# A causal convolution and a spectral mix: seven weight groups ahead, tail channels of two batches on two row tiles, T copies on two engines, one store per row block of four batches

## The chip, the cores and the metric

The kernel runs on one core of a Trainium2 chip. The metric is the device time of one launch in microseconds. Before, it was 216.48 us in the median of three runs, from 214.84 to 218.25. The profiled execution took 218.14 us as a run and spans 216.4 us from its first to its last instruction.

## The reference

```python
# x: (8, 3264, 192) f32; weight: (8, 7); moe_w_r, moe_w_i: (64, 192, 192); moe_w_ch: (192, 192)
w = softmax(weight, axis=-1)
x_unf = zero_pad_front(x, 6)[:, idx, :].reshape(B, S, 7, 8, 24)
x = einsum('hk,bskhg->bshg', w, x_unf).reshape(B, S, D)       # causal convolution over seven rows
X = rfft(x, axis=1)[:, :64]
Y = X @ (w_r + 1j * w_i)                                      # one 192 x 192 matrix for each of 64 modes
u = x + irfft(Y, n=S, axis=1)
out = u + maximum(u @ w_ch, 0)
```

Both Fourier transforms are done as matmuls with matrices of sines and cosines, since only 64 modes are kept.

## The kernel before

The sequence of 3264 rows is cut into 27 windows of 122 rows; a tile has 128 partitions, of which 122 are a window's own rows. `x_all` holds all eight batches and all windows in bf16. The program is written out in the order in which each engine shall work; no scheduler moves it.

**First stage, to about 75 us.** POOL's queue loads x, 24 loads (L63), casting to bf16, and behind them `w_ch` and the first weight groups. For each batch and each third of its windows `conv_unit` convolves with a banded matrix on PE (L237) and copies back into `x_all` on ACT (L244) or DVE (L246). `dft_unit` (L296) sums the 64 modes over the windows, and `xtrans` (L308, two column tiles of 64) turns the result for the mixing, into `xt`.

**Second stage, to about 121 us.** The 64 modes are mixed in 16 groups of four (loop at L367). A group's weights `wt`, real and imaginary, are two loads of 288 KB (L221) from POOL into a pool of three buffers. For each g, twelve matmuls on four column tiles (L373) give `yp`, ACT copies it to `ymix` (L379), POOL is told to load group g+3 into the buffer that has come free, then `t_next` puts one or two T units on PE and DVE, and the two transposes `et` (L387) and DVE's copy (L388) write `yeT`.

A T unit turns a third of a batch's `x_all` so that channels lie on partitions, as the last stage needs it, into `cT`. The 192 channels don't fit 128 partitions: slots alternate between channels 0 to 127 of one window, of the next, and a slot with the 64 tail channels of both, which `make_tail` (L253 to L256, DVE) has copied side by side. Up to eight transposes (L283) fill a PSUM tile, and DVE copies it out (L285), twice per unit. 24 units are spread by `2 - g % 2` over the groups, and what is left is done after g = 14 (L390), ahead of the last mix. `g_part` (L348, ACT L349) does the same for the inverse transform's matrix `gst`.

**Last stage.** For each pair of batches `zwi_pair` multiplies `yeT` by `win0` and `win1`, whose first 192 columns are `w_ch` and whose last 192 are the identity. `group_z` forms u @ w_ch for two windows and two batches in a PSUM tile of two banks (`zp`): two matmuls of 384 columns from `gst` (L422), four of 192 columns from the main channels (L427), four from the tail channels (L429). The tail matmul contracts over all 128 rows, half of which meet the zeros in `wB0` or `win1`. ACT applies the relu in place (L432). Two groups later `group_y` adds y = irfft(Y) by two more matmuls (L437) and DVE adds x (L441) into `t`, from a pool of four. A `t` has four windows of two batches, so two groups, and SP stores it, one store for each batch (L456). Windows overlap by six rows of which a later store brings the right values, so the last round's rows are cut exactly, into two pieces each. There are 80 stores; SP waits for the eighth before to land.

Of the kernel before, what the change touches and what calls it, by code (L numbers as in the profile page):

```python
# [18 lines left out]
def kernel(  # L19
# [9 lines left out]
    nc = tc.nc  # L29
# [11 lines left out]
    PAIRS = NWIN // 2  # L41
    NSLOT = 3 * PAIRS + 2
# [7 lines left out]
    USLOTS = ((0, 15), (15, 12), (27, 14))  # L50
# [35 lines left out]
    cband = ep.tile([P, H, P], BF16, tag="cband")  # L86
    fst = ep.tile([P, NWIN, 2 * MODES], BF16, tag="fst")
    xt = ep.tile([P, 4, 2 * B, MODES], BF16, tag="xt")
    sel = ep.tile([P, 2, P], BF16, tag="sel")
# [125 lines left out]
    wp = early_stack.enter_context(tc.tile_pool(name="wts", bufs=3, side="right"))  # L215
    wtiles = {}

    def load_weights(g):
        wt = wp.tile([P, MG, 3, D], BF16, tag="wt", name="wt")
        for half, src in ((0, moe_w_r), (1, moe_w_i)):  # L220
            nc.gpsimd.dma_start(out=wt[64 * half:64 * half + 64, :, :, :],  # L221
                                in_=src[MG * g:MG * g + MG, :, :].rearrange("m (p j) e -> p m j e", j=3))
        wtiles[g] = wt

    for g in range(3):
        load_weights(g)
    workp = early_stack.enter_context(tc.tile_pool(name="work", bufs=2, side="right"))
# [20 lines left out]

    def make_tail(b, u):
        w0, n = UNITS[u]  # L250
        tl = workp.tile([P, 10, D - P], BF16, tag="tail")
        if u < 2:
            nc.vector.tensor_copy(out=tl[0:WIN, 0:n, :], in_=x_all[0:WIN, b, w0:w0 + n, P:D])  # L253
        else:
            nc.vector.tensor_copy(out=tl[0:WIN, 0:n - 1, :], in_=x_all[0:WIN, b, w0:w0 + n - 1, P:D])
            nc.vector.tensor_copy(out=tl[0:WIN, n - 1:n + 1, :], in_=x_all[0:WIN, b, w0 + n - 2:w0 + n, P:D])  # L256
        return tl

    def slot_lhsT(b, u, tl, slot):
        i, r = divmod(slot, 3)  # L260
        w0 = UNITS[u][0]
        if i == PAIRS:
            if r == 0:
                return x_all[0:WIN, b, NWIN - 1, 0:P]
            j = NWIN - 1 - w0
        elif r < 2:
            return x_all[0:WIN, b, 2 * i + r, 0:P]
        else:
            j = 2 * i - w0
        return tl[0:WIN, j:j + 2, :].rearrange("p w e -> p (w e)")  # L270

    def slot_of(w):
        if w == NWIN - 1:
            return NSLOT - 2, NSLOT - 1, 1
        return 3 * (w // 2) + w % 2, 3 * (w // 2) + 2, w % 2

    def t_unit(b, u, tl):
        s0, n = USLOTS[u]
        h1 = (n + 1) // 2
        for a, cnt in ((s0, h1), (s0 + h1, n - h1)):  # L280
            tp = ptr.tile([P, 8 * WIN], BF16, tag="tp")
            for k in range(cnt):
                nc.tensor.transpose(tp[:, WIN * k:WIN * k + WIN], slot_lhsT(b, u, tl, a + k),  # L283
                                    ident[0:WIN, 0:WIN])
            nc.vector.tensor_copy(out=cT[:, b, WIN * a:WIN * (a + cnt)], in_=tp[:, 0:WIN * cnt])  # L285

    xps = {}

    def dft_unit(b, u):
# [8 lines left out]
        if u == 2:  # L298
            xs = workp.tile([P, D], BF16, tag="xs")
            nc.vector.tensor_copy(out=xs[:], in_=xp[:, 0:D])  # L300
            xps[b] = xs
# [15 lines left out]
    for i, (b, u) in enumerate(units):  # L317
        conv_unit(i, b, u)
        if i == 2:
            make_f()  # L320
            setup_stack.close()
        if xq:
            xtrans(xq.pop(0))
        dq.append((b, u))
        lag = max(1, 5 - i // 4)
        while len(dq) > lag:
            db, du = dq.pop(0)
            dft_unit(db, du)
            if du == 2:
                xq.append(db)  # L330
# [7 lines left out]
    stashp = ctx.enter_context(tc.tile_pool(name="stash", bufs=1))  # L338
    cT = stashp.tile([P, B, CTW], BF16, tag="cT")
    nc.vector.memset(cT[:, :, NSLOT * WIN:CTW], 0.0)  # L340


    def g_part(g):
        tp = ptr.tile([P, 8 * WIN], BF16, tag="tp")
        c0 = 8 * g
        n = min(8, NWIN - c0)
        for k in range(n):
            nc.tensor.transpose(tp[:, WIN * k:WIN * k + WIN], fst[0:WIN, c0 + k, :], ident[0:WIN, 0:WIN])  # L348
        nc.scalar.copy(out=gst[:, WIN * c0:WIN * (c0 + n)], in_=tp[:, 0:WIN * n])  # L349


    NG4 = MODES // 4
    tunits = [(b, u) for b in range(B) for u in range(3)]
    tails = [make_tail(*tunits[0])]
    tpos = [0]

    def t_next():
        i = tpos[0]
        if i == len(tunits):
            return  # L360
        tpos[0] += 1
        if i + 1 < len(tunits):
            tails.append(make_tail(*tunits[i + 1]))
        t_unit(*tunits[i], tails[i])

    gq = list(range((NWIN + 7) // 8))
    for g in range(NG4):  # L367
        yp = pconv.tile([P, 512], F32, tag="cv", name="yp")
        for j in range(3):
            for pos in range(4):  # L370
                m = 4 * g + pos
                wt = wtiles[m // MG]
                nc.tensor.matmul(yp[32 * pos:32 * pos + 32, 0:D],  # L373
                                 xt[:, j:j + 2, :, m].rearrange("p j k -> p (j k)"), wt[:, m % MG, j, :],
                                 start=(j == 0), stop=(j == 2), tile_position=(0, 32 * pos))
        if g + 3 < NGRP:
            load_weights(g + 3)
        ymix = workp.tile([P, D], BF16, tag="ymix")
        nc.scalar.copy(out=ymix[:], in_=yp[:, 0:D])  # L379
        for _ in range(2 - g % 2):  # L380
            if g < NG4 - 1:
                t_next()
        if gq and g % 2 == 1:
            g_part(gq.pop(0))
        et = pxx.tile([P, 2, P], BF16, tag="xt", name="et")
        for t in range(2):
            nc.tensor.transpose(et[:, t, :], ymix[:, 64 * t:64 * t + P], ident[:])  # L387
        nc.vector.tensor_copy(out=yeT[:, :, 4 * g:4 * g + 4, :],  # L388
                              in_=et[:, :, :].rearrange("p t (q k) -> p t q k", q=4)[:, :, :, 0:16])
        if g == NG4 - 2:  # L390
            while tpos[0] < len(tunits):
                t_next()
    early_stack.close()
    ps1.close()


    p3 = ctx.enter_context(tc.tile_pool(name="p3", bufs=4, side="right"))
    zwip = ctx.enter_context(tc.tile_pool(name="zwip", bufs=1, side="right"))
    zwi = zwip.tile([P, B, 2, D], BF16, tag="zwi")
    pz = ctx.enter_context(tc.tile_pool(name="pz", bufs=4, space=PSUM))  # L400

    def zwi_pair(q):
        zp = pz.tile([P, 2, 512], F32, tag="z", name="zwps")
        for i in range(2):
            b = 2 * q + i
            nc.tensor.matmul(zp[:, i, 0:2 * D], yeT[:, 0, :, :].rearrange("p m (c b) -> p (m c) b", c=2)[:, :, b], win0[:], start=True, stop=False)
            nc.tensor.matmul(zp[:, i, 0:2 * D], yeT[:, 1, :, :].rearrange("p m (c b) -> p (m c) b", c=2)[:, :, b], win1[:], start=False, stop=True)
        for i in range(2):
            dst = zwi[:, 2 * q + i, :, :]
            srcv = zp[:, i, 0:2 * D].rearrange("p (t d) -> p t d", t=2)  # L410
            if i == 0:
                nc.vector.tensor_scalar(out=dst, in0=srcv, scalar1=ascale[:, 0:1], scalar2=None, op0=ALU.mult)
            else:
                nc.scalar.activation(out=dst, in_=srcv, func=ACT.Copy, scale=ascale[:, 0:1])  # L414

    wBs = (wB0[:, :], win1[:, 0:D])

    def group_z(q, ws):
        zp = pz.tile([P, 2, 512], F32, tag="z")
        for k, w in enumerate(ws):  # L420
            sa, sb, par = slot_of(w)
            nc.tensor.matmul(zp[:, k, 0:2 * D], gst[:, WIN * w:WIN * w + P], zwi[:, 2 * q:2 * q + 2, 0, :],  # L422
                             start=True, stop=False, skip_group_check=True)
            for i in range(2):
                b = 2 * q + i
                o = zp[:, k, D * i:D * i + D]
                nc.tensor.matmul(o, cT[:, b, WIN * sa:WIN * sa + P], win0[:, 0:D], start=False, stop=False,  # L427
                                 skip_group_check=True)
                nc.tensor.matmul(o, cT[:, b, WIN * sb:WIN * sb + P], wBs[par], start=False, stop=(i == 1),  # L429
                                 skip_group_check=True)  # L430
        n = len(ws)
        nc.scalar.activation(out=zp[:, 0:n, 0:2 * D], in_=zp[:, 0:n, 0:2 * D], func=ACT.Relu)  # L432
        return zp

    def group_y(q, ws, zp, t, k0):
        for k, w in enumerate(ws):
            nc.tensor.matmul(zp[:, k, 0:2 * D], gst[:, WIN * w:WIN * w + P], zwi[:, 2 * q:2 * q + 2, 1, :],  # L437
                             start=False, stop=True, skip_group_check=True)
        n = len(ws)
        step = ws[1] - ws[0] if n > 1 else 1  # L440
        nc.vector.tensor_tensor(  # L441
# [79 lines left out]
```

## Time and profile before

| stage | us | what is busy |
|---|---|---|
| convolution, DFT | 0 to 75 | transfers, 192 GB/s to 70 us |
| mixing, T transposes | 75 to 121 | transfers, 200 GB/s to 117 us |
| start of the last stage | 121 to 140 | PE 13.3 of 20 us |
| steady last stage | 140 to 190 | PE without a gap, 300 GB/s |
| last stores | 190 to 216.4 | 223 to 254 GB/s |

| group of instructions | count | mean ns |
|---|---|---|
| L427, L429 matmul, 192 columns | 432 | 249 |
| L422, L437 matmul, 384 columns | 216 | 331, 326 |
| L283 transpose | 328 | 223 |
| L285 DVE copy of T, both of a unit's halves counted | 48 | 588 |
| L349 ACT copy of gst, 976 columns | 3 | 972 |
| L432 ACT relu of a group | 52 | 795 |
| L441 DVE add of a group | 52 | 958 |
| L456 store | 80 | 432 on SP (median) |

Matmuls are pipelined: a matmul's time is its whole way through the array, and the next one starts after its columns have streamed, every 0.082 us for 192 columns. In the granted clock a 1.00 is full speed.

### The profile page before, as it was taken

The numbers are of one execution on the slowest core, as the hardware profiler recorded it, in microseconds if no ns is written. First come the engines' busy times: TensorE is split into PE (matmuls) and PEld (weight loads), VectorE is DVE, ScalarE is ACT, GpSimd is POOL, SyncE is SP. The second block draws the span as 40 slices with busy tenths as digits, with TensorE's granted clock in tenths as the row PEclk, the third lists the DMA queues.
The fourth block names the chain that finished last, engine by engine and source line by source line (L and its number), as shares of the span: only waits on it lengthen the run. The fifth ranks groups of instructions, "written<-read, shape, count | busy, mean of one in ns | idle before, by whom it ended". The sixth has DMA issues, their size and how long they took to land.

```text
span 216.4 us, 4281 instructions
## 1 busy us (share of the span) xinstructions
PE 164.1 (76%) x1706; PEld 129.4 (60%) x1706; DVE 127.2 (59%) x224; ACT 95.9 (44%) x145; POOL 53.7 (25%) x89
## 2 busy tenths in 40 slices
PE   0248489889889798786666577799999999998700
PEld 0005267869768577665555455578878877786500
DVE  7876416433344478775767414477777777777520
ACT  2693954466547213311001144466665556665400
POOL 8998533434232044442440000000000000000000
PEclk9999999999999979999999879999999999999975
DMA  2999999999999389999998002559999999986795
GB/s 22 151 174 192 192 191 194 190 193 193 193 195 177 66 113 175 192 201 206 208 199 140 0 0 65 175 168 299 301 303 292 303 303 299 304 261 203 208 256 143
DMA packets 65669, 41.35 MB, mean 191 GB/s; under 512 B 30241, under 2 KB 65649, under 8 KB 65649
## 3 DMA queue, kind: packets, MB, share of 16 engines
q0 software_dynamic: 37088, 20.14, 68.8%
q1 hardware_dynamic: 28560, 20.94, 32.2%
q8 instruction: 13, 0.21, 0.4%
q14 instruction: 8, 0.06, 0.1%
HBM read 40.31 MB, written 20.90 MB: 283 GB/s over the span
## 4 chain that ended last, share of the span: by engine, by line
PE 50%; DMA 13%; DVE 13%; ACT 10%; SPq 6%; issue 3%; POOL 1%; DVEq 0%; ACTq 0%
DMA wt<-in_moe_w_i_dram 13%; PE cp L237 8%; PE zp L422 7%; PE zp L427 7%; PE zp L429 7%; PE xp L296 6%; PE zp L437 6%; SPq L456 6%; DVE x_all L246 4%; ACT scaled L175 4%; PE tp L283 3%; ACT x_all L244 3%; PE yp L373 2%; DVE t L441 2%; DVE cT L285 2%
## 5 line engine op out<-in xcount | busy, mean ns | idle before, releaser
L441 DVE TENSOR_TENSOR t<-zp,x_all 128x768 f32<-128x768 f32 (+1 forms) x56 | 51.6, 928 | 25.7 <-PE zp L437 23.0
L432 ACT ACTIVATE zp<-zp 128x768 f32<-128x768 f32 (+1 forms) x56 | 43.2, 772 | 33.2 <-PE zp L429 33.1
L427 PE MATMUL zp<-win,cT 128*128 128x192 bf16 x216 | 45.2, 249 | 0.0
L422 PE MATMUL zp<-zwi,gst 128*128 128x384 bf16 x108 | 35.7, 331 | 7.1 <-ACT zwi L414 5.9
L244 ACT CAST x_all<-cp 122x768 bf16<-122x768 f32 (+2 forms) x32 | 26.9, 878 | 23.6 <-PE cp L237 22.9
L237 PE MATMUL cp<-x_all,cband 128*128 128x240 bf16 (+2 forms) x192 | 27.8, 288 | 7.9 <-DVE x_all L232 3.2
L285 DVE COPY cT<-tp 128x854 bf16<-128x854 bf16 (+2 forms) x48 | 26.3, 588 | 11.2 <-PE tp L283 10.6
L246 DVE CAST x_all<-cp 122x960 bf16<-122x960 f32 (+2 forms) x16 | 17.0, 1064 | 22.7 <-PE cp L237 22.7
L237 PEld LDWEIGHTS <-cband 128*128 128x128 bf16 x192 | 19.5, 109 | 15.0 <-issue 7.0
L427 PEld LDWEIGHTS <-cT 128*128 128x128 bf16 x216 | 21.4, 99 | 11.9 <-issue 8.7
L63 POOL DMA_DIRECT2D x_all<-in_x_dram x24 | 23.9, 1005 | 15.5 <-DMA x_all<-in_x_dram 15.5
L437 PE MATMUL zp<-zwi,gst 128*128 128x384 bf16 x108 | 26.6, 326 | 0.0
L429 PEld LDWEIGHTS <-cT 128*128 128x128 bf16 x216 | 21.4, 99 | 7.3 <-issue 0.5
L283 PE MATMUL tp<-ident,x_all 122*128 122x122 bf16 x216 | 22.4, 223 | 2.9 <-DVE cT L285 2.6
L296 PE MATMUL xp<-x_all,fst 122*128 122x192 bf16 (+1 forms) x216 | 23.0, 256 | 0.9 <-DVE x_all L246 0.5
L429 PE MATMUL zp<-win,cT 128*128 128x192 bf16 x112 | 23.3, 248 | 0.0
L429 PE MATMUL zp<-wB,cT 128*128 128x192 bf16 x104 | 21.9, 250 | 0.0
L283 PEld LDWEIGHTS <-x_all 122*128 122x128 bf16 x216 | 17.3, 100 | 6.5 <-issue 4.0
L379 ACT CAST ymix<-yp 128x192 bf16<-128x192 f32 x16 | 5.1, 320 | 35.5 <-PE yp L373 35.5
L283 PE MATMUL tp<-ident,tl 122*128 122x122 bf16 x112 | 20.5, 223 | 0.0
L296 PEld LDWEIGHTS <-fst 122*128 122x128 bf16 (+1 forms) x216 | 18.9, 102 | 2.2 <-DVE x_all L246 0.7
L221 POOL DMA_DIRECT2D wt<-in_moe_w_r_dram x16 | 9.8, 616 | 33.9 <-PE yp L373 27.8
(81 smaller groups left out, 154.8 us busy)
## 6 DMA issues: line engine op xcount, KB each, us to landing
out_dram<-t SPq DMA_DIRECT2D x40, 384.0 KB, 2.7
wt<-in_moe_w_r_dram POOLq DMA_DIRECT2D x16, 288.0 KB, 6.3
wt<-in_moe_w_i_dram POOLq DMA_DIRECT2D x16, 288.0 KB, 7.1
x_all<-in_x_dram POOLq DMA_DIRECT2D x8, 432.0 KB, 14.6
x_all<-in_x_dram POOLq DMA_DIRECT2D x9, 384.0 KB, 18.1
x_all<-in_x_dram POOLq DMA_DIRECT2D x7, 480.0 KB, 17.8
out_dram<-t SPq DMA_DIRECT2D x8, 288.0 KB, 2.4
out_dram<-t SPq DMA_DIRECT2D x8, 252.0 KB, 3.1
```

What stands on the lines that cost most here:

```text
L237: nc.tensor.matmul(cp[:, j, 0:GRP * n].rearrange("p (w e) -> p w e", w=n), cband[:, h, :], x_all[:, b, w0:w0 + n, GRP * h:GRP * h + GRP], ...
L244: nc.scalar.copy(out=dst, in_=srcv)
L246: nc.vector.tensor_copy(out=dst, in_=srcv)
L283: nc.tensor.transpose(tp[:, WIN * k:WIN * k + WIN], slot_lhsT(b, u, tl, a + k), ident[0:WIN, 0:WIN])
L285: nc.vector.tensor_copy(out=cT[:, b, WIN * a:WIN * (a + cnt)], in_=tp[:, 0:WIN * cnt])
L296: nc.tensor.matmul(xp[:, 0:D], fst[0:k, c, :], x_all[0:k, b, c, :], start=(c == 0), stop=(c == NWIN - 1))
L422: nc.tensor.matmul(zp[:, k, 0:2 * D], gst[:, WIN * w:WIN * w + P], zwi[:, 2 * q:2 * q + 2, 0, :], start=True, stop=False, skip_group_check ...
L427: nc.tensor.matmul(o, cT[:, b, WIN * sa:WIN * sa + P], win0[:, 0:D], start=False, stop=False, skip_group_check=True)
L429: nc.tensor.matmul(o, cT[:, b, WIN * sb:WIN * sb + P], wBs[par], start=False, stop=(i == 1), skip_group_check=True)
L432: nc.scalar.activation(out=zp[:, 0:n, 0:2 * D], in_=zp[:, 0:n, 0:2 * D], func=ACT.Relu)
L437: nc.tensor.matmul(zp[:, k, 0:2 * D], gst[:, WIN * w:WIN * w + P], zwi[:, 2 * q:2 * q + 2, 1, :], start=False, stop=True, skip_group_check ...
L441: nc.vector.tensor_tensor(out=t[:, k0:k0 + n, :].rearrange("p k (b e) -> p k b e", b=2), in0=zp[:, 0:n, 0:2 * D].rearrange("p k (b e) -> p ...
```

## The change

**Weights.** The convolution's constants get a pool of their own on the right side, freed after the first stage. The room of the setup's tiles, free after the third convolution unit, takes the T matrix of three pairs of batches (`cTa`) and a pool for four weight groups (`wts0`); with the three rotating buffers seven groups are asked for behind x. After g = 3 the four are freed for the fourth pair's matrix (`cTb`); from g = 4 on, group g+3 is loaded when mix(g) has read its buffer.

**Tail channels.** A T matrix now belongs to a pair of batches, b and b+2. It has 27 slots with the main channels of b, 27 of b+2, and 27 in which partitions 0 to 63 hold b's tail channels and 64 to 127 those of b+2. In the last stage the two are contracted as two tiles of 64 rows, each writing its own PSUM bank. The matmuls against zeros are gone.

**T copies.** A call of `t_next` does two chunks of seven or eight transposes; DVE copies the first out, ACT the second; the same for `gst`. Both, and the mixing's tiles, use one pool of four PSUM buffers. 22 calls fill g = 0 to 14.

**Last stage.** A group is one window and four batches, so that a finished `t` is one store. There are eight `t` buffers, each half as big. 54 groups, 60 stores. The first two groups' products that don't need the mixing are put ahead of its last transposes; the y and w_ch parts of the mix are made one by one, ahead of and between the first groups.

The core of the diff:

```diff
+            for g in range(4):
+                load_weights(g, wp0)
+            for g in range(4, 7):
+                load_weights(g, wp)
...
+    def t_next(avail):
...
+        for h in range(2):
+            p, k0, n = chunks[i + h]
+            tp = pt.tile([P, 1024], BF16, tag="p", name="tp")
+            for k in range(n):
+                nc.tensor.transpose(tp[:, WIN * k:WIN * k + WIN], slot_lhsT(p, k0 + k),
+                                    ident[0:WIN, 0:WIN])
+            dst = cTs[p][:, WIN * k0:WIN * (k0 + n)]
+            if h == 0:
+                nc.vector.tensor_copy(out=dst, in_=tp[:, 0:WIN * n])
+            else:
+                nc.scalar.copy(out=dst, in_=tp[:, 0:WIN * n])
...
-        if g + 3 < NGRP:
-            load_weights(g + 3)
...
+        for i in range(2):
+            for k in range(2):
+                p = 2 * h + i
+                c0 = WIN * (2 * NWIN + w)
+                nc.tensor.matmul(zp[:, k, D * i:D * i + D], cTs[p][64 * k:64 * k + 64, c0:c0 + P], wBs[k],
+                                 start=False, stop=(i == 1 and not first), skip_group_check=True,
+                                 tile_position=(64 * k, 0))
...
+        for r0, r1 in rows:
+            dst = bass.AP(tensor=out.tensor, offset=out.offset + (4 * h * S + WIN * w + r0) * D,
+                          ap=[[D, r1 - r0], [S * D, B // 2], [1, D]])
+            nc.sync.dma_start(out=dst, in_=t[r0:r1, :, :])
...
+        if g == 3:
+            wts0_stack.close()
+            cTb = ctx.enter_context(tc.tile_pool(name="stashb", bufs=1)).tile([P, CTW], BF16, tag="cTb")
+            nc.vector.memset(cTb[:, NSLOT * WIN:CTW], 0.0)
+            cTs[3] = cTb[:, :]
+        if 4 <= g and g + 3 < NGRP:
+            load_weights(g + 3, wp)
+        if not last:
+            for _ in range(1 + g % 2):
+                t_next(2 if g < 3 else 3)
+            if gq and g % 2 == 0:
+                g_part(gq.pop(0))
+        else:
+            zps = [pza.tile([P, 2, 512], F32, tag="z", name="z") for _ in range(2)]
+            for n in range(2):
+                group_ab(*seq[n], zps[n], True)
+        mix_t(g, *m)
...
+    zw_part(0, 0)
+    zw_part(0, 1)
+    for n in range(2):
+        group_g(*seq[n], zps[n], 0, False, False)
+        relu(zps[n])
+    for n in range(2):
+        zw_part(1, n)
+        finish_group(*seq[n], zps[n])
```

## The prediction, made before the changed kernel was run

> **What bounds the kernel now.** I read the slices of the page first, then the waits, the queue that issues the weights, the windows, and last the PE timeline where a tiling mode changes.
>
> ```profile
> GB/s 22 151 174 192 192 191 194 190 193 193 193 195 177 66 113 175 192 201 206 208 199 140 0 0 65 175 168 299 301 303 292 303 303 299 304 261 203 208 256 143
> ...
> q0 software_dynamic: 37088, 20.14, 68.8%
> q1 hardware_dynamic: 28560, 20.94, 32.2%
> ```
>
> A slice is 5.41 us. The row shows three stages. Up to 72 us transfers run near 192 GB/s (x, then three weight groups) while PE convolves. From 75 to 118 us thirteen more weight groups stream at about 200 GB/s, beside the T transposes. From 133 us only stores run, at about 302 GB/s. Between them lie two holes: 70 to 78 us, and 117 to 133 us, in which nothing moves at all.
>
> ```profile
> POOL wt L221 <- PE yp L373: 27.8, 12, 9.3
> ...
> PE yp L373 <- DMA wt<-in_moe_w_i_dram: 6.3, 6, 1.4
> ```
>
> ```profile
> 65.75 0.64 POOL L221 DMA_DIRECT2D wt<-in_moe_w_i_dram  x1
> 75.66 0.61 POOL L221 DMA_DIRECT2D wt<-in_moe_w_r_dram  x1 [9.26 <-PE yp L373]
> ```
>
> The first hole is the longest wait of that list: the fourth group is issued 9.26 us after the third, because its buffer is the first group's, which mixing reads at 74.8 us. From then on PE waits for weights, and POOL for PE to free a buffer.
>
> ```profile
> 72.00:74.00 2.00, 1.14 (x15) 0.91 (x15) 0.71 (x2) 0.00 (x0) 0.00 (x0) 1.00 0.13 21
> 74.00:76.00 2.00, 1.34 (x27) 1.10 (x22) 1.01 (x4) 0.32 (x1) 0.34 (x1) 0.86 0.04 8
> 76.00:78.00 2.00, 1.96 (x21) 1.76 (x18) 1.78 (x5) 0.00 (x0) 0.88 (x2) 0.50 0.44 15
> ...
> 150.00:160.00 10.00, 10.00 (x95) 8.12 (x94) 7.44 (x8) 6.07 (x8) 0.00 (x0) 1.00 0.99 301
> 160.00:170.00 10.00, 10.00 (x94) 8.00 (x93) 7.18 (x9) 6.20 (x8) 0.00 (x0) 1.00 0.99 305
> ...
> 190.00:205.00 15.00, 13.75 (x118) 10.06 (x115) 10.20 (x13) 8.26 (x12) 0.00 (x0) 1.00 0.76 223
> ```
>
> In these windows (PE, PEld, DVE, ACT, POOL busy, clock, DMA share, GB/s) the last stage is bound twice: PE is busy 10.00 of 10 us and the DMA engines 0.99 of it. From 190 us neither is full any more (0.76, 223 GB/s): the chain of waits there consists of SPq L456, the issue of 40 small stores at some 0.5 us each. PE's last matmul ends at 204.95 us, the span at 216.4, so 11.4 us of stores hang over.
>
> ```profile
> 176.20 0.16 PE zp L422
> ...
> 177.19 0.33 PE zp L437 x2
> ...
> 178.50 0.33 PE zp L437 x2
> ```
>
> The chain of waits gives the pace: L437 comes back every 1.31 us. Of this, 0.33 are the two of L437, 0.33 the two of L422, and eight matmuls of 192 columns take 0.082 each, 0.66.
>
> **What the Trainium skill says.** "TensorEngine Tiling (Array Packing)", Key Properties: tiles of one mode run in parallel, but changing the tiling mode drains TensorE. The kernel before has such changes, at the two-column-tile L308 (start, length):
>
> ```profile
> 36.46 0.49 PE L237 MATMUL cp<-x_all,cband 128*128 128x192 bf16 x4
> 36.88 0.38 PE L308 MATMUL tp<-sel,xs 128*64 128x128 bf16 x6
> 37.19 0.59 PE L296 MATMUL xp<-x_all,fst 122*128 122x192 bf16 x5
> ```
>
> The trace agrees on both. Four matmuls at 0.082 should have streamed by 36.79; L308 starts at 36.88: 0.09 us lost. L308's six span 0.38 - 0.23 (one's mean) = 0.15 us from first start to last, where an unpaired pitch of 0.053 (128 columns) would need 0.27: pairs do overlap. The last starts at 37.03, has streamed by 37.08, and L296 starts at 37.19: 0.11. At 41.8 us the same two changes lose 0.14 and 0.12. So one change costs 0.09 to 0.14 us. Row tiles are not shown by this trace.
>
> "DMA: Bandwidth & Descriptors", Anatomy of one DMA — SWDGE (gpsimd) path: about 2 us fixed per DMA. The trace agrees: issued at 75.66, the fourth group shows no rate until about 77.8 us.
>
> **The change, part by part.**
>
> *Seven groups prefetched.* POOL issues the seven behind x, so the queue runs on after 72.3 us. A group is 2 x 288 KB, at 200 GB/s 2.95 us: group 6 lands at 72.3 + 4 x 2.95 = 84.1 us. Then there is nothing to load until mix(4) frees the first of the three rotating buffers. Before, mix(4) ran at 86.08 us unhindered by weights, with 98 transposes ahead of it since 74.8. After, 6 x 15 + 27 = 117 stand ahead, but copies are shared. The memset of cTb on DVE waits for all seven groups (84.1), and behind it DVE's T copies of g=3 are queued, which PE needs for free PSUM: mix(4) cannot run before about 85.3. I take 86 (bounds 85.3 and 90). Group 7 then flows from 86.5 + 2.1 = 88.6 us, and nine groups take 26.6: the last lands at 115.2. The hole has moved, from 72.3–77.8 to 84.1–88.6, and is only about 2 us smaller (before, the last landed near 117.2). So the title item is worth 2 us.
>
> *T copies on two engines.* Before, a unit cost DVE two copies, 2 x 0.588 = 1.18, plus 0.3 for the tail. Now DVE copies one half (0.6) and ACT the other (a gst copy of 976 columns on ACT takes 0.97; 854 some 0.86). From mix(4) on this lies beside the weights (2.95 per group, for 1.5 calls of 0.9 on ACT and 0.8 of transposes on PE) and pays nothing, save at the end: before, leftover units stood between mix(14) at 115.95 and mix(15) at 120.0. Now none is left over after g=14: mix(15) starts at about 115.5. With the 2 us above this is 4.5 us earlier.
>
> *Start of the last stage.* Before, mix(15) at 120.0 leads to the first t at 132.17 and the first store at 133.20: the four zwi pairs come in a chain with their evacuations. After: mix 0.45; two groups' products from cT put ahead, 2 x 1.1 (they delay the et transposes by some 1.4, but are work taken off later); et and yeT 0.9; first zw part 0.35; evacuations on DVE and ACT 0.6 each, 1.35 with their waits; relu 0.8 and y 0.45; t 1.0. Sum 7.5: first store at 123.2, ten us earlier than before. Group 2 waits for the old PSUM buffers (the last zw evacuation on ACT) and starts PE at about 124.
>
> *Tail channels on two row tiles.* Streams per group: 4 x 0.163 + 4 x 0.082 = 0.98, and four tail matmuls in two pairs, at least 0.16; their four weight loads at 0.053 (the pitch of the transposes) give 0.21, which I take. But every group changes mode twice, 128 rows to 64 and back: 2 x 0.115 = 0.23 (0.18 to 0.28 by the trace). Pace 0.98 + 0.21 + 0.23 = 1.42 us, against 1.31: the pairing saves 0.12 and pays 0.23. 52 groups at 1.42 end at 197.8 us. DVE's 0.958 and ACT's 0.795 per group stay below this.
>
> *One store per row block.* Bytes and 768 byte pieces stay the same, so the DMA pace stays at 20.94 MB / 302 GB/s = 69.3 us for 54 groups, 1.28 each: under PE's 1.42, so stores keep up. Issues fall from 80 to 60, and the last nine groups hold 15 of them (15 x 0.43 = 6.5 us in 12.7). The overhang shrinks from 11.4 us to relu 1.0 + y 0.5 + t 1.05 + two issues 0.9 + landing 2.3 + end 2.0 = 7.7.
>
> Sum: 197.8 + 7.7 = 205.5 us of span. A run differs from its span by some 1.7 us (218.14 against 216.4), as much as the runs differ among themselves, and the median of before, 216.48, equals its span, so I leave it at 205.5.
>
> **Rivals.** *The stores become the bound.* If PE hides the mode changes, its pace is about 1.2 and the DMA's 1.28 to 1.30 sets the end: 124 + 52 x 1.30 + 7.7 = 199. For it: the share of 0.99 at 302 GB/s today, and an array that may treat row tiles more gently than column tiles. Against: four changes of four that I looked at lost time.
>
> *Slower mixing.* Mixing, four T or gst chunks and the et transposes of one g rotate through four PSUM buffers, so at odd g et waits for ACT's last copy, and the next mix stands behind it on PE. If mix(4) slips to 90, all later weights slip by 4: 209. For it: PE strictly in order; against: ACT needs only 8.3 us for its work before mix(4).
>
> *The change costs a full drain.* If a change exposes a matmul's tail (0.249 - 0.08 = 0.17) and a weight load (0.10), it costs 0.27, and without any pairing the four tails take 0.33: pace 0.98 + 0.33 + 0.54 = 1.85; with pairing 1.73. At 1.73: 124 + 52 x 1.73 + 7.7 = 222, slower than now. For it: twice per group, 104 times; against: the 0.09 to 0.14 measured, for column tiles.
>
> **How the numbers follow.** Forecast 205.5: 0.52. Stores bound, 199: 0.27. Slower mixing, 209: 0.12. Full drain, 222: 0.09. The predicted time is the forecast's. The range leaves the drain out and goes from 196 (199, with a start 3 us earlier) to 212 (209, or a change at 0.14 with group 2 at 126 instead of 124: 210, and some more). Faster by over 2% means below 212.2: the first three cases but for 0.05, so 0.86. Within 2%: 0.07. Slower by over 2%: most of the drain case, 0.07.
>
> **What would show it.** Group 6 landing near 84 and a second hole up to 88 to 89 us; mix(4) near 86; mix(15) near 115.5; the first store near 123; y matmuls 1.42 us apart, with two gaps of about 0.1 us around the tail matmuls, and a DMA share near 0.9. A pace of 1.30 with the share at 0.99 is the stores' case, one above 1.6 the drain. I am wrong if PE waits for weights at other places than g=7 and after, or if ACT, now with copies, becomes what the transposes wait for.

## The result, and the profile after

The changed kernel takes 206.57 us in the median of four runs (205.81 to 208.6), the kernel before 216.77 in the same comparison: a ratio of 0.957, 95% interval 0.946 to 0.968. The forecast was 205.5, with a range from 196 to 212. The profiled execution is the slowest of the four (208.6 us, a span of 206.9). Ratios, here and below, compare undisturbed executions alone; of three kernels below, about half of whose executions fell into a slower state, only the ratio is given.

The slices of the page, after (a slice is 5.17 us):

```profile
GB/s 20 156 165 191 192 192 192 192 192 194 193 190 201 206 206 202 11 116 205 206 175 176 158 1 50 153 269 292 291 296 284 293 292 284 303 290 276 273 284 143
```

Transfers now run on without a gap to 83 us, then nearly stop for more than a slice (11 GB/s). Later slices of the weights reach 175, 176 and 158 where before there were 199 to 208. The empty stretch before the stores is shorter.

The list of waits, and the queue of POOL, the seventh group's second half and the eighth group's first:

```profile
POOL wt L223 <- PE yp L396: 27.6, 9, 14.8
...
PE yp L396 <- DMA wt<-in_moe_w_i_dram: 4.9, 4, 2.2
```

```profile
72.50 0.61 POOL L223 DMA_DIRECT2D wt<-in_moe_w_i_dram  x1 [0.22 <-issue]
87.88 0.61 POOL L223 DMA_DIRECT2D wt<-in_moe_w_r_dram  x1 [14.77 <-PE yp L396]
```

The one long wait of POOL for PE is still there, 14.77 us instead of 9.26, only later. In total POOL waits as long as before (27.6 against 27.8).

Windows of after (PE, PEld, DVE, ACT, POOL busy, clock, DMA share, GB/s). The first three lie in the mixing, the fourth at the start of the last stage, the last in its steady part:

```profile
96.00:98.00 2.00, 0.27 (x5) 0.09 (x2) 0.60 (x2) 1.13 (x2) 0.00 (x0) 1.00 1.21 203
98.00:105.00 7.00, 6.27 (x76) 5.42 (x80) 2.70 (x6) 2.70 (x5) 2.43 (x4) 0.56 1.21 205
113.00:119.00 6.00, 5.53 (x63) 4.50 (x64) 3.19 (x7) 2.38 (x4) 0.00 (x0) 0.50 0.98 161
120.00:140.00 20.00, 18.81 (x179) 11.69 (x179) 10.23 (x14) 11.05 (x17) 0.00 (x0) 1.00 0.42 128
...
150.00:160.00 10.00, 10.00 (x92) 5.67 (x89) 7.20 (x8) 5.62 (x8) 0.00 (x0) 1.00 0.95 289
```

PE is as full as before in the steady part, but the DMA share has fallen from 0.99 to 0.95: stores no longer bind, PE alone does. In the mixing PE's clock is at half speed for two long stretches, 98.8 to 105.7 us and 112.5 to 119.3, after a shorter one at 75 us that the kernel before has too. From 120 to 140 us PE is busy 18.81 us; before it was

```profile
120.00:140.00 20.00, 13.27 (x105) 10.00 (x105) 7.06 (x11) 7.42 (x11) 0.00 (x0) 0.91 0.18 54
```

The chain of waits of after, two groups of the steady part, and then PE's timeline through one group's change of mode and back:

```profile
160.08 0.76 PE z L458 x4
160.83 0.33 PE z L446 x4
161.44 0.76 PE z L458 x4
```

```profile
160.92 0.25 PE L446 MATMUL z<-win,cTb 128*128 128x192 bf16 x1
161.10 0.25 PE L452 MATMUL z<-wB,cTa 64*128 64x192 bf16 x1
161.10 0.25 PE L452 MATMUL z<-win,cTa 64*128 64x192 bf16 x1
161.19 0.24 PE L452 MATMUL z<-wB,cTb 64*128 64x192 bf16 x1
161.19 0.24 PE L452 MATMUL z<-win,cTb 64*128 64x192 bf16 x1
161.37 0.34 PE L458 MATMUL z<-zw,gst 128*128 128x384 bf16 x1
```

Groups are 1.36 us apart instead of 1.31. The two row tiles do start together (161.10 twice), and the second pair 0.09 later: four matmuls take the time of two. But the last full matmul has streamed by 161.00 and the tiles start at 161.10; they have streamed by 161.27 and the next full one starts at 161.37. Each change of mode costs 0.10 us.

**Where the 10 us came from.** The last mix, mix(15), starts at 119.86 us, against 119.94 before: the second stage, which the weights and the T copies are about, gave nothing between these two executions. All of the difference lies behind mix(15):

| | before | after |
|---|---|---|
| mix(15) starts | 119.94 | 119.86 |
| first store, after mix(15) | 13.3 | 7.7 |
| last matmul ends, after mix(15) | 85.0 | 79.6 |
| span ends, after the last matmul | 11.5 | 7.4 |
| span ends, after mix(15) | 96.5 | 87.0 |

I use the last line as a measure of the last stage, since it doesn't contain the mixing's scatter: in the three experiments below that leave the last stage as it is, it is 86.9, 87.0 and 86.7.

But the two executions are not alike in PE's clock: between 70 us and mix(15) it was at half speed for 3.4 us before and for 17.1 us after. Four kernels below leave the second stage as the change made it, so their traces are further executions of it:

| kernel | at half clock, us | mix(4) | mix(15) |
|---|---|---|---|
| each store cut in two | 3.4 | 85.40 | 116.33 |
| zw parts first | 6.8 | 85.82 | 117.43 |
| four changes of mode | 10.6 | 87.00 | 119.43 |
| tails over all 128 rows | 13.7 | 87.10 | 119.63 |
| the changed kernel | 17.1 | 87.03 | 119.86 |

The longer the slow clock, the later mix(15). In the first row, with as long a slow stretch as before had, mix(15) starts 3.6 us earlier than before. So the second stage seems to have gained as well, and the slow clock to have taken the gain back in the changed kernel's trace. These are single executions, and longer waits of PE could be the reason for both columns.

### The profile page after: what moved, and what is told of

It reads as the page before. It is cut to its first block, busy times and chain, and to the rows that moved or that the text cites. A ratio compares the mean times of both kernels' runs of the same rounds, so it can differ in the third digit from the quotient of the medians.

```text
span 206.9 us, 4292 instructions
## 1 busy us (share of the span) xinstructions
PE 167.5 (81%) x1722; PEld 118.2 (57%) x1722; DVE 118.1 (57%) x185; ACT 112.9 (55%) x163; POOL 53.6 (26%) x89
## 4 chain that ended last, share of the span: by engine, by line
PE 59%; DMA 12%; DVE 12%; ACT 10%; issue 3%; POOL 1%; DVEq 1%; ACTq 0%
PE z L458 19%; DMA wt<-in_moe_w_i_dram 12%; PE cp L235 8%; PE z L446 8%; PE z L452 7%; PE xp L255 7%; DVE x_all L244 4%; ACT scaled L177 4%; PE tp L363 4%; ACT x_all L242 3%; PE yp L396 2%; DVE t L471 1%; PE tp L267 1%; PE zwps L419 1%; ACT fst L190 1%
## 5 line engine op out<-in xcount | busy, mean ns | idle before, releaser
L471 DVE TENSOR_TENSOR t<-z,x_all 128x768 f32<-128x768 f32 x54 | 51.5, 957 | 23.0 <-PE z L458 22.2
L462 ACT ACTIVATE z<-z 128x768 f32<-128x768 f32 x54 | 42.8, 795 | 29.9 <-PE z L452 29.9
L458 PE MATMUL z<-zw,gst 128*128 128x384 bf16 x216 | 45.2, 328 | 0.9 <-DVE zw L430 0.7
L458 PEld LDWEIGHTS <-gst 128*128 128x128 bf16 x216 | 16.8, 98 | 16.8 <-issue 9.1
L446 PE MATMUL z<-win,cTa 128*128 128x192 bf16 x162 | 24.4, 246 | 0.0
L369 ACT COPY cTa<-tp 128x854 bf16<-128x854 bf16 (+1 forms) x16 | 14.4, 909 | 9.2 <-PE tp L363 9.2
L223 POOL DMA_DIRECT2D wt<-in_moe_w_r_dram x16 | 9.9, 619 | 32.5 <-PE yp L396 27.6
L367 DVE COPY cTa<-tp 128x854 bf16<-128x854 bf16 (+1 forms) x17 | 10.6, 626 | 13.2 <-PE tp L363 12.9
L446 PEld LDWEIGHTS <-cTa 128*128 128x128 bf16 x162 | 15.0, 98 | 5.2
L452 PE MATMUL z<-win,cTa 64*128 64x192 bf16 x81 | 15.9, 249 | 0.0
L452 PE MATMUL z<-wB,cTa 64*128 64x192 bf16 x81 | 15.9, 250 | 0.0
```

What stands on the lines that cost most here:

```text
L369: nc.scalar.copy(out=dst, in_=tp[:, 0:WIN * n])
L446: nc.tensor.matmul(zp[:, k, D * i:D * i + D], cTs[p][:, c0:c0 + P], win0[:, 0:D], start=False, stop=False, skip_group_check=True)
L452: nc.tensor.matmul(zp[:, k, D * i:D * i + D], cTs[p][64 * k:64 * k + 64, c0:c0 + P], wBs[k], start=False, stop=(i == 1 and not first), ski ...
L462: nc.scalar.activation(out=zp[:, :, 0:2 * D], in_=zp[:, :, 0:2 * D], func=ACT.Relu)
L471: nc.vector.tensor_tensor(out=t[:].rearrange("p (k i) e -> p k i e", k=2), in0=zp[:, :, 0:2 * D].rearrange("p k (i e) -> p k i e", i=2), i ...
```

## The experiments

All are compared with the kernel before on the same chip. Times are medians; the changed kernel stands at 206.57.

**Tails over all 128 rows.**

```diff
-    wBs = (wB0[0:64, :], win1[64:P, 0:D])
+    wBs = (wB0[:, :], win1[:, 0:D])
...
-                nc.tensor.matmul(zp[:, k, D * i:D * i + D], cTs[p][64 * k:64 * k + 64, c0:c0 + P], wBs[k],
+                nc.tensor.matmul(zp[:, k, D * i:D * i + D], cTs[p][:, c0:c0 + P], wBs[k],
```

> The changed kernel, with the tail channels contracted over all 128 rows against zeros again instead of on two tiles of 64 rows; all else stays. Theory (the two changes of tiling mode in each group, about 0.10 us each, cost more than the pairing saves): y matmuls 1.31 us apart instead of 1.358, DMA share up to 0.98 or 0.99, 52 x 0.048 = 2.5 us less: about 204 us. Rival (the pairing halves the tail work and is a gain): two more streams of 0.082 per group, 1.52 us apart, about 215 us.

203.83 us, ratio 0.944 (0.937 to 0.951). From the chain of waits:

```profile
163.34 0.33 PE z L446 x4
163.67 0.33 PE z L452 x4
164.00 0.65 PE z L457 x4
164.65 0.33 PE z L446 x4
```

Groups are 1.31 us apart, with no gap between the forms, and the last stage takes 84.3 us instead of 87.0. The rival's 215 us is out: the two row tiles lose 2.7 us.

**Four changes of mode in a group.**

```diff
-        for k in range(2):
-            for i in range(2):
+        for i in range(2):
+            for k in range(2):
                 p, r = 2 * h + i, k
...
-        for i in range(2):
             for k in range(2):
                 p = 2 * h + i
                 c0 = WIN * (2 * NWIN + w)
```

> The changed kernel with the tail matmuls of a group done in two pairs, each behind its own two main matmuls, so four changes of tiling mode in a group instead of two; the same matmuls. Theory (a change of mode costs about 0.10 us of PE, whatever is loaded): y matmuls 1.358 + 0.20 = 1.56 us apart, 52 x 0.2 = 10 us more, about 217 us. Rival (the loss comes with the loading of 64-row weights, not with the change): the pace stays at 1.36 to 1.40, 207 to 209 us.

One execution, 223.15 us. The same matmuls, the same weight loads. The chain, one group (L451 is the tail, 0.19 for a pair, L446 two main matmuls and the gaps around them):

```profile
162.47 0.76 PE z L457 x4
163.22 0.17 PE z L446 x2
163.39 0.19 PE z L451 x2
163.58 0.27 PE z L446 x2
163.85 0.19 PE z L451 x2
164.04 0.76 PE z L457 x4
```

A group takes 1.57 us, 0.21 more for two more changes, 0.105 each. So it is the change and not the weights of 64 rows. 52 x 0.21 are 10.9 us; the further 4 us lie between mix(15) and the first store (11.9 us), where PE ran at half its clock in this execution.

**Three weight groups ahead instead of seven.**

```diff
-            for g in range(4):
-                load_weights(g, wp0)
-            for g in range(4, 7):
+            for g in range(3):
                 load_weights(g, wp)
...
-        if 4 <= g and g + 3 < NGRP:
+        if g + 3 < NGRP:
```

> The changed kernel with three weight groups asked for ahead as before the change, group g+3 loaded after every mix(g), and a T matrix of its own for the fourth pair from the start; all else stays. Theory (seven ahead only move the hole in the weight stream): the hole lies at 72 to 78 us instead of 83 to 89, thirteen groups after it end near 117 us, and the time is within 2 us of the changed kernel: 205 to 209 us. Rival (the prefetch is what shortens the second stage): the stream loses the 11 us that the four groups filled, about 217 us.

206.48 us, ratio 0.956 (0.949 to 0.963): no difference from the changed kernel. Its slices show the hole back at its old place and none at 84 us:

```profile
GB/s 20 157 158 191 192 192 192 193 192 195 191 192 184 200 17 163 196 205 206 201 197 203 144 0 91 151 281 285 281 306 290 292 288 265 321 290 277 260 293 149
```

mix(15) starts at 117.43, with 3.4 us at half clock; with seven groups and as long a slow stretch it was 116.33. The prefetch moves the hole, and what it is worth, at most 1 us by these two traces, does not show in the time.

**Mixing first.**

```diff
-            for _ in range(1 + g % 2):
-                t_next(2 if g < 3 else 3)
+            for _ in range(2 if g >= 4 else 0):
+                t_next(3)
```

> The changed kernel with no T units between the first four mixes, and two calls after each of g = 4 to 14 instead of one and two by turns from g = 0; same number of calls. Theory (the hole at 83 to 89 us is there because mix(4), which frees the first buffer, stands behind six calls of T work): mix(4) near 80 to 82 us, no hole, last weights at 110 to 111 us, mix(15) at 111 to 114, about 199 us. Rival (PE's T work bounds the second stage, whatever its order): mix(15) stays at 118 to 120 us, 205 to 208 us.

203.3 us, ratio 0.939 (0.933 to 0.946), between the two. mix(4) runs at 82.17 instead of 87.03, the eighth group is issued at 83.22, and mix(15) starts at 114.29, 5.6 us earlier than in the changed kernel's trace; the last stage is unchanged (87.0). The hole was indeed due to the T work in front of mix(4). But I had put the last weights at 110 to 111 and 199 us; from mix(4) to mix(15) it now takes 32 us, 2.9 per group. Of the 5.6 us a part may be the slow clock of the changed kernel's trace; the medians differ by 3.3.

**All T copies on DVE.**

```diff
-            if h == 0:
+            if h < 2:
                 nc.vector.tensor_copy(out=dst, in_=tp[:, 0:WIN * n])
```

> The changed kernel with all T and gst copies on DVE, none on ACT; all else stays. Theory (T copies are beside the weight stream, except ahead of mix(4), where they delay the freeing of the first buffer): six calls and two gst parts ahead of mix(4) get up to 5 us longer on DVE, of which 2 to 4 reach mix(4), the hole and the end: 208 to 211 us. Rival (the copies are hidden altogether): 206 to 207 us.

207.96 us, ratio 0.964 (0.956 to 0.971); the changed kernel's interval overlaps it. mix(4) is at 86.64, which looks no later than the 87.03 of the changed kernel's trace. But there PE was at half clock from 74.9 to 78.4 us, and here it was not; the two traces of the same second stage at full clock up to mix(4) have 85.40 and 85.82. Against these, copies on DVE alone delay mix(4) by 0.8 to 1.2 us, and mix(15), at 118.53, comes 2.2 us later than in the cut stores' trace, which has as long a slow stretch (3.4 us). So the path of the theory is there, but smaller than the 2 to 4 us that it reckoned. That sharing the copies gains time, 1.4 us by the medians, is likely and not shown.

**Each store cut in two.**

```diff
-            nc.sync.dma_start(out=dst, in_=t[r0:r1, :, :])
+            for i in range(2):
+                dst = ...two batches
+                nc.sync.dma_start(out=dst, in_=t[r0:r1, 2 * i:2 * i + 2, :])
```

> The changed kernel with each store cut into two, one for each two batches: 120 stores of half the size instead of 60; all else stays. Theory (one store per block pays only where SP's issue is the bound, in the last rounds with their exact rows): pace and DMA share of the steady part as before the cut, the last nine groups hold 30 issues of some 0.4 us, 12 us, as long as these groups last on PE, so 0 to 2 us more: 206.5 to 208.5 us. Rival (half the stores is what brought the last stage forward): SP issues 120 x 0.4 = 48 us in place of 24 and waits for the eighth before, DMA share below 0.9 all along, 210 us or more.

207.7 us, ratio 0.960 (0.953 to 0.966), 1.1 more than the changed kernel. The groups keep their 1.36 us; SP's 120 issues take 0.468 each in the median. The last stage is 89.8 us, 2.8 longer: more than the 2 us of the theory, and of its kind, at the end: the steady pace does not suffer.

**Zw parts first at the start of the last stage.**

```diff
-            for n in range(2):
-                group_ab(*seq[n], zps[n], True)
         mix_t(g, *m)
...
     zw_part(0, 0)
     zw_part(0, 1)
+    zw_part(1, 0)
+    zw_part(1, 1)
+    for n in range(2):
+        group_ab(*seq[n], zps[n], True)
```

> The changed kernel with the old order at the start of the last stage: the first two groups' products are not put ahead of the last et transposes but behind the zw parts, and all four zw parts are made before the first group; the zeros that open the banks come from a tile of their own. Theory (order at this point is worth the idle time of PE that it fills): PE idles some 0.6 us for ymix and some for the evacuations, 1.3 us of zw matmuls come before the first store, which leaves 10 to 11 us after mix(15) instead of 7.7; of these 2 to 3 us, 1 to 2 stay in the end: 207.5 to 208.5 us. Rival (the stores have slack to catch up): the time stays at 206 to 207.

206.44 us, ratio 0.951 (0.944 to 0.959): no change in the time, as the rival had it. In the trace the first store comes 10.8 us after mix(15), as the theory said, and the last stage takes 88.3, 1.3 more. This execution's mix(15) was at 117.43, 2.4 us earlier than in the changed kernel's trace, so the medians say little here. PE was also at half clock from 118.6 to 122.1 us, so the order by itself is worth 1.3 us at most. Nor is this order the whole old start: the kernel before made each of four `zwi` pairs directly ahead of its own two groups, and here all parts are made ahead of the first group.

**Full rows and mixing first in one.**

> The two edits that were faster in one: tails over all 128 rows, no T units between the first four mixes, and the gst parts after g = 5 and 7 instead of 0 and 2. Theory (stages add up, and mix(4) now stands behind nothing but four mixes of 1.5 us): mix(4) near 80.5 us, before the seventh group has landed at 83, so no hole; last weights at 110, mix(15) at 110 to 113, first store at 118 to 120, pace 1.31: 198 to 200 us. Rival (T work is the bound from g = 4 on, at 2.9 us per g, and the stores are at their limit): mix(15) stays at 114, and 201 us or more.

The diffs of these two, and the `gst` parts after g = 5 and 7. 200.94 us, ratio 0.927 (0.922 to 0.932), faster than with either edit alone. POOL issues the eighth group at 81.88, before the seventh has landed, and there is no hole:

```profile
81.88 0.61 POOL L223 DMA_DIRECT2D wt<-in_moe_w_r_dram  x1 [6.93 <-PE yp L396]
```

mix(4) is at 80.83, as expected. But mix(15) is at 115.14: from g = 4 on a group takes 3.1 us, more than its weights (2.95); the first of them took 4.0, at half clock until 84.5 us, the others 3.0. From 85 to 115 us PE is busy for 26.2 of 30 us. Stages add up, and the second one is now bound by PE, by T work in the main, as the rival said.

**T chunks in idle PSUM banks.** Four banks are set aside for the last stage. Three kernels put T chunks there, both of a call in one tile of two banks: the kernel with full rows and mixing first, the same with one T call ahead of mix(4), and the changed kernel.

```diff
+        tz = pza.tile([P, 2, 512], F32, tag="z", name="tz")
         for h in range(2):
             p, k0, n = chunks[i + h]
-            tp = pt.tile([P, 1024], BF16, tag="p", name="tp")
+            tp = tz[:, h, :].bitcast(BF16)
```

> The faster combination (tails over all 128 rows, first four mixes without T units, gst parts after g = 5 and 7), with the T chunks in the four PSUM banks that are set aside for the last stage and idle until then, instead of the pool of four that they share with the mixing. Theory (from g = 4 on PE waits inside the rotation of the four buffers: et for ACT's last copy, T chunks for free banks): about 2.5 us of PE per g, less than the 2.95 us of weights, last weights at 110, mix(15) at 111 to 112.5, 197.5 to 199 us. Rival (the wait is for DVE's tail copies and for the engines' order, not for banks): mix(15) stays at 114 to 115, 200 to 201 us.

> The same, with one of the two T calls of g = 14 moved to g = 3. Theory: mix(4) at about 82, still before the seventh group has landed (83), and one call (1 us) less between mix(14) and mix(15): 0 to 1 us less than the kernel beside it. Rival: POOL's 2 us from issue to flow open a hole, 0 to 1 us more.

> The changed kernel with only this edit: T chunks in the idle banks. Theory (mix(4) stands behind the rotation too): mix(4) at 84 to 85.5 instead of 85.4 to 87, so a hole shorter by 1 to 2 us and as much off the time: 204.5 to 206 us. Rival (tails and order): 206 to 207 us.

All three were far slower than expected by either theory: ratios to before of 1.011 (1.001 to 1.021), 1.018 (1.009 to 1.027) and 0.983 (0.974 to 0.991), where with the old buffers the first has 0.927 and the third 0.957 (the second was not run with them). They test something else than was meant. PE's timeline of the first of them, the second chunk of a call:

```profile
104.91 0.59 PE L364 MATMUL tz<-ident,x_all 122*128 122x122 bf16 x8 [0.69 <-DVE cTa L368]
```

The second chunk's transposes stand behind DVE's copy of the first, since both are the same tile: a new wait of 0.7 us per call on PE. The trace has it 22 times, once per call, 15.8 us in all; mix(15) comes 16.2 us later than with the old buffers. The slow clock has a part in that too, 20.5 us at half speed against 6.8. The question was put again with a tile for each chunk:

```diff
+    ptx = psx.enter_context(tc.tile_pool(name="ptx", bufs=4, space=PSUM))
...
-            tp = pt.tile([P, 1024], BF16, tag="p", name="tp")
+            tp = ptx.tile([P, 1024], BF16, tag="x", name="tp")
```

> The faster combination again, with the T chunks in four single-bank tiles of a pool of their own in the banks that are idle until the last stage. The three kernels before this put both chunks of a call into one tile of two banks, so that the second chunk's transposes waited for DVE's copy of the first (0.7 us on PE per call); here no chunk shares a tile. Theory (PE waits inside the rotation of the four shared buffers): about 2.5 us of PE per g, last weights at 110 us, mix(15) at 111 to 112.5, 197.5 to 199 us. Rival (the wait is for DVE's tail copies and the order of the engines): mix(15) at 114 to 115, 200 to 201 us.

199.95 us, ratio 0.927 (0.924 to 0.930): the same ratio as without it. mix(15) is at 114.71, where the rival had it (114 to 115). The rotation of the four shared buffers is not what holds PE. What PE waits for in its trace is, in part, DVE's copy of the tail channels, which is queued there behind T copies:

```profile
105.08 1.07 PE L364 MATMUL tp<-ident,tail 122*128 122x122 bf16 x14 [0.85 <-DVE tail L324]
```

From mix(4) to mix(15) there are five such waits, 3.3 of 34 us; for the most part PE is at work, 25.2 of 29 us from 86 us on, and at half clock before. An earlier tail copy was not tried, so that it would help is argued and not shown; these waits hold 3.3 us and no more.

## Why the prediction was right, and where its steps were not

*Seven groups prefetched: right that the hole moves, not shown that it shrinks.* It lies from 83.2 to 89.3 us (forecast 84.1 to 88.6), 6.1 us long where it was 5.5 before. mix(4) ran at 87.03 (forecast 86); without the slow clock at 75 us it is at 85.4 and 85.8 in two other traces. Three groups ahead give the same time. A step on the way was wrong: the memset of `cTb` does not wait for all seven groups. In the cut stores' trace it runs at 82.65 us, while the transfers go on to about 84, and in the changed kernel's trace directly behind the copy ahead of it. What stands in front of mix(4) is T and `gst` work. And the prediction's 2 us from POOL's issue to the flow are not the fixed cost that the Trainium skill's "DMA: Bandwidth & Descriptors" (Anatomy of one DMA) describes: that page puts most of its 2 us behind the last byte. What these traces show is 1.3 us from the start of the issue to the first packet, at 76.97 before and 89.18 after.

*"mix(15) starts at about 115.5": wrong here, by 4.4 us.* The step that failed is that T work from mix(4) on "lies beside the weights" and "pays nothing". PE was taken at full clock. In the windows shown, PE waits for weights from 96 to 98 us and does next to nothing, and then runs at 0.56 and at 113 to 119 us at 0.50 of its clock. From mix(13) at 113.32 to mix(14) at 117.50, with two calls between, it takes 4.2 us; with the zw parts first, where the clock is full at this point, 3.1. In the kernel with the cut stores, whose second stage is the same program, the clock stays at full speed from 98 to 105, and mix(15) starts at 116.33:

```profile
98.00:105.00 7.00, 4.24 (x79) 3.49 (x82) 3.82 (x9) 3.79 (x6) 2.54 (x5) 1.00 1.21 205
...
116.33 0.54 PE L396 MATMUL yp<-wt,xt 128*32 128x192 bf16 x12 [0.17 <-DMA wt<-in_moe_w_i_dram]
```

This is within 1 us of the forecast. That the slow clock is the cause of the rest is drawn from the five traces of the table above; no run set the clock alone. A slow stretch also delays the next issue of weights, which fits the dip of their rate later.

*Start of the last stage: right.* Forecast 7.7 us from mix(15) to the first store (its terms add up to 7.5), measured 7.7. Group 2 starts on PE 8.25 us after mix(15), forecast 8.5.

*Tail channels: right in kind, sizes off.* The pairing was said to save 0.12 and the changes of mode to cost 0.23. Four tails take 0.17 instead of 0.21, the two changes 0.20 instead of 0.23. The pace is 1.36 instead of 1.42, 52 x 0.06 = 3.1 us less; and the first three of these groups go at 1.03, since no y matmuls come between them yet, about 0.8 less, which the forecast left out. The full rows confirm the loss with 2.7 us.

*The overhang: 7.7 forecast, 8.9 measured* from the last group's tail matmuls (198.0 us) to the end of the span. Three adds of DVE stand in a row there, 2.7 us, where one of 1.05 was reckoned; the last `t` is done at 201.3 instead of 200.6.

So the span came out at 206.9 instead of 205.5 because terms cancelled: +4.4 in the second stage, -0.3 at the start, -3.9 in the groups, +1.2 at the end. In part that is luck: the slow clock and the pace have nothing to do with each other.

*Small misreadings.* In the first hole of before, "nothing moves at all" is too strong: the windows shown have 8 to 21 GB/s. And mix(15) of before starts at 119.94, not 120.0. Neither bears on the sum.

*The rivals.* The stores did not become the bound (share 0.95). With full rows they are near it: 0.94 to 1.03 in that kernel's windows. The full drain is out, at 0.10 per change. Slower mixing, 209 us, was right in that the second stage was late by about 4 us, and wrong in its reason: mix(4) was late by 1 us only.

What is not settled: where the 9.5 us come from that the last stage gained. 4.1 of them lie behind the last matmul and 5.4 ahead of it. For the 5.4, the windows from 120 to 140 us have 5.5 us more of PE work after, and the lists of waits, first before and then after, name what PE stood for:

```profile
PE zp L422 <- ACT zwi L414: 5.9, 4, 1.6
...
PE z L458 <- DVE zw L430: 0.7, 1, 0.7
```

Before, each of the four `zwi` pairs stood directly ahead of its own groups, DVE copied one half and ACT the other after it, and PE waited 1.3 to 1.6 us each time. After, only one wait of 0.7 is left. The clock of before was also at half from 123.2 to 126.7 us. Against these gains stand 52 x 0.05 = 2.6 us of slower pace. So the traces point to the four waits as the largest part; no run put them back, so it is not shown. The new shape of a group, one window and four batches, was not undone alone either. Of the 4.1 at the end, stores cut in two lose 2.5 there, but they are half as large as the full stores of before (192 KB, 384), so that run is no return to the old stores, and this part stays open too.

## What to carry to other kernels

A deeper prefetch pays only if the buffers that it waits for next also come free earlier: look at what stands in front of the first reader, here six calls of T work, and move that (mixing first gained 3.3 us, four more buffers none; mixing first with three buffers was not run). Two row tiles that save 0.16 us of streams and need two changes of mode at 0.10 us are a loss; a change needs more than that between it and the next. Before the banks are split among engines, see that two chunks don't share a tile, since the second then waits for the first one's copy. And before two traces are compared stage by stage, compare their clocks: here a slow stretch hid a gain of some 3 us in one comparison and a delay of about 1 us in another.

## What was not expected of the hardware

PE's clock fell to half without a long wait. In the changed kernel it fell at 74.9, 98.8 and 112.5 us. These are the 3.4 us ahead of each fall:

```profile
71.52:74.93 3.41, 1.81 (x30) 1.25 (x27) 1.56 (x6) 0.07 (x1) 1.22 (x2) 1.00 1.21 207
95.42:98.83 3.41, 1.55 (x32) 1.27 (x30) 0.98 (x3) 1.77 (x3) 0.49 (x1) 1.00 1.21 206
109.07:112.48 3.41, 1.77 (x34) 1.33 (x30) 1.35 (x4) 2.33 (x4) 1.22 (x2) 1.00 1.15 180
```

PE was busy for 1.55 to 1.81 us of each, about half, and the longest idle time inside them was 0.66, 1.86 and 1.35 us. The Trainium skill's "TensorE: Matmul & The Clock Gate" (What's actually happening) puts the half-rate clock after at least one idle window of about 3.4 us. If idle means that nothing runs, the measurement differs: here half-filled stretches were enough. How full one must be to keep the clock was not tested. And the same second stage ran with the clock at half for 3.4 to 17.1 us in different executions, with mix(15) starting at 116.33 to 119.86 us.
